# An mLSTM cell and a SwiGLU block on one core: scores and state products in one segment at a seam, and a mask by maximum

## The chip, the core and the metric

The kernel runs on one core of a Trainium2 chip. The core has a matrix engine (TensorE, PE in the profile; its weight loads are PEld), a vector engine (VectorE, DVE), an activation engine (ScalarE, ACT), a general engine (GpSimd, POOL) and a queue engine that issues DMAs (SyncE, SP). Each engine runs its own instructions in order, and semaphores order them between engines. The metric is the time of one execution in microseconds, as the median of several.

## The reference

An mLSTM cell runs over 768 time steps for 4 batches and 8 heads with 40 features a head, and its output is the input of a gated feed-forward block with 320 inputs and 1536 hidden units. Everything is in 32-bit floats, except the weights, which come as 64-bit floats.

```python
for t in range(S):                                   # cell
    m_new = maximum(f[t] + m, i[t])
    f_stab = exp(f[t] + m - m_new);  i_stab = exp(i[t] - m_new);  m = m_new
    C = f_stab * C + i_stab * outer(v[t], k[t])
    n = f_stab * n + i_stab * k[t]
    y[t] = sigmoid(o[t]) * (C @ q[t]) / max(|n . q[t]|, 1)
g = x @ w_gate                                       # block, x = y as (tokens, 320)
out = (g * sigmoid(g) * (x @ w_val)) @ w_out
```

## The kernel before

**The cell in stretches of 64 steps.** The recurrence is cut into sub-stretches of 64 steps. Inside one, the weight of key s for query t is a matrix: w = exp(g_s - M_t) for s up to t and 0 beyond, with g from the gates and M a running maximum. Then y is (scores * w) times v, plus the state from before, decayed. Two sub-stretches make a group of 128 steps, and there are six groups, each of 512 tokens (128 steps of 4 batches). For the cell of a group the kernel needs:
- the weights w: `weights_load` spreads M over w_sb by DMA (L476), `weights_sub` subtracts it from g on VectorE (L483), `weights_mask` writes -1e30 where s > t with an affine select on POOL (L488), and `weights_exp` takes the exponential on ScalarE (L492);
- `weigh_values` (L363, POOL): the values v times the last column of w, into vw_sb;
- kT and qT, keys and queries with features on partitions. For groups 2 on they are made from "squares": sixteen DMAs (`load_squares`, L336) bring k or q in squares of 32, and VectorE turns these in place (`turn_squares`, L342);
- `do_scores` (L352): 64 products of kT and qT; `do_weigh` (L359, VectorE) multiplies them by w;
- `do_add` (L378): 64 products of k_sb and vw_sb, what a sub-stretch adds to the state; `do_state` adds it (L394, VectorE), between decays of the state on POOL (L387, `do_decayed` for the first);
- `do_attend` (L401 and L406) and `do_gather` (L415 on): products with the state and with the values, summed and divided; `do_divide` and `send_squares` bring the result as squares to x_sq, where `turn_inputs` makes xT, the block's input.

**The block in two phases for each group.** From group 1 on, `gated` makes the hidden units in six chunks k of two blocks of 128. A seven-product scheme replaces eight block products, so there are sums of weights (`weight_sums`, made once, in group 1) and sums of inputs (`input_sums`, kept in q_sb). A chunk has products into a PSUM tile gv_x, then some into gv_y, then the rest into gv_x; `second(k - 1)` finishes the chunk before. `project_seven` then makes the outputs with seven products in steps 0 to 7. Group 0 goes another way: `hidden` for twelve blocks, and `project_all` with a list of things to do after each (`after`).

**The order is written out by hand.** While the block of group g runs, the cell of group n = g + 1 is computed and group f = g + 2 is loaded. The dictionary `at` says what is issued after which part of a chunk: "a" follows the first part of gv_x, "b" stands before gv_y, "c" behind gv_y, "d" at the chunk's end. So on TensorE `do_add` stands behind chunk 0 and `do_scores` behind chunk 1. `between(g)` does the same for the steps of `project_seven`. Each engine's queue follows this order.

**PSUM in four pairs.** From group 1 on, PSUM is four pairs of banks, handed out in turn: `take` takes the next free pair, and a pair goes back to the end of the list where the code says that its reader has been issued. gv_x and gv_y take one pair each, scores two, state products two. A product into a pair waits until the readers of its last use are through.

**Memory used twice.** x_sq holds the squares of the inputs, and its first part, under the name k_sq, the squares of k. POOL clears it once (`memset` in group 1). In group 0 the squares of k go to a tile of their own, "raw" (`early_squares`).

Of the kernel before, what the change touches and what calls it, by code (L numbers as in the profile page):

```python
# [9 lines left out]
F32 = mybir.dt.float32  # L10
# [3 lines left out]
AF = mybir.ActivationFunctionType  # L14
ALU = mybir.AluOpType
# [4 lines left out]
SUB = 64  # L20
NEG = -1e30
# [3 lines left out]
def kernel(  # L25
# [18 lines left out]
    nc = tc.nc  # L44
# [13 lines left out]
    UH = BH // 2  # L58
# [6 lines left out]
    const = ctx.enter_context(tc.tile_pool(name="const", bufs=1))  # L65
# [31 lines left out]
    def half(i):  # L97
        return slice(i * SUB, (i + 1) * SUB)
# [5 lines left out]
    def heads(P):  # L104
        return slice(P * UH, (P + 1) * UH)

    k_sb = const.tile([128, BH, DP], F32)
# [3 lines left out]
    w_sb = const.tile([128, BH, SUB], F32)  # L111
    vw_sb = const.tile([128, BH, D1], F32)
    kT = const.tile([128, PP, L], F32)
    qT = const.tile([128, PP, L], F32)
# [6 lines left out]
    g_T = const.tile([128, NG, BH], F32)  # L121
    e_T = const.tile([128, NG, BH], F32)
    dec = const.tile([128, NS - 2, PP], F32)
    tmp = const.tile([128, 3 * TW], F32)
    sw0 = const.tile([128, 3, 2, 128], F32)
    ident = early.tile([128, 128], F32)
    f0 = early.tile([128, L], F32)
    i0 = early.tile([128, L], F32)
# [215 lines left out]
    q_sq = q_sb.rearrange("p (a x) d -> p a (x d)", x=2).rearrange("p a (t d) -> p a t d", d=SQ)  # L344
# [3 lines left out]
    def scores(P):  # L348
        sp = [x.rearrange("p (a t) -> p a t", t=SUB) for x in duo("sp")]
        for a in range(UA):  # L350
            for two, i in QUAD:
                nc.tensor.matmul(sp[two][half(i), a, :], lhsT=kT[feats(two), P * UA + a, half(i)],  # L352
                                 rhs=qT[feats(two), P * UA + a, half(i)], start=True, stop=True)
        return sp

    def weigh(P, sp):
        w2 = w_sb[:, heads(P)].rearrange("p (a two) t -> p two a t", two=2)
        for two in range(2):
            nc.vector.tensor_tensor(w2[:, two], sp[two], w2[:, two], op=ALU.mult)  # L359
        give("sp", P)  # L360
# [11 lines left out]
    def add(n, P):  # L372
        ps = smalls("add")
        rows, w = (half, DP) if n == 1 else (feats, D)
        for a in range(UA):
            for i, two in QUAD:
                h = P * UH + 2 * a + two
                nc.tensor.matmul(ps[i][rows(two), a, :], lhsT=k_sb[half(i), h, 0:w], rhs=vw_sb[half(i), h, :],  # L378
                                 start=True, stop=True)
        return ps  # L380
# [104 lines left out]
    def weights_mask(P):  # L485
        for i in range(2):
            w = w_sb[half(i), heads(P)]
            nc.gpsimd.affine_select(w, w, compare_op=ALU.is_ge, fill=NEG, base=0, pattern=[[0, UH], [1, SUB]],  # L488
                                    channel_multiplier=-1)

    def weights_exp(P):
        nc.scalar.activation(w_sb[:, heads(P)], w_sb[:, heads(P)], AF.Exp)  # L492
# [13 lines left out]
    A, V, G = nc.scalar, nc.vector, nc.gpsimd  # L506
# [383 lines left out]
    def do_scores():  # L890
        for P in range(2):
            live["sp", P] = scores(P)

    def do_weigh(P):
        weigh(P, live.pop(("sp", P)))

    def do_add(n):
        for P in range(2):
            live["add", P] = add(n, P)
# [29 lines left out]
    def load_all(dst, a, n):  # L929
        for P in range(2):  # L930
            load(dst, a, n, P)

    run = lambda f, *a, **b: (lambda: f(*a, **b))
# [9 lines left out]
        1: [run(piece_load, 6), run(late_decay)],  # L943
        2: [run(nc.scalar.activation, step1, step1, AF.Exp), run(decay_rows), run(weights_load, 1), run(load_all, v_sb, v, 1)],
        3: [run(late_turns)],
        4: [run(decay)],
        5: [run(turn, 0, (A, A), (A, V))],
        6: [run(turn, 1, (A, A), (A, V)), run(piece_load, 7)],
        7: [run(weights_sub, 1, 0), run(weights_mask, 0), run(weights_sub, 1, 1), run(weights_mask, 1), run(nc.gpsimd.memset, q_sb, 0.0)],
        8: [run(weights_exp, 0), run(weights_exp, 1), run(weigh_values, G, 0), run(weigh_values, G, 1),  # L950
            run(piece_load, 8)],
# [11 lines left out]
    def early_squares(part):  # L963
# [10 lines left out]
        2: [run(do_divide, 1, 0), run(convert, 15)],  # L974
        3: [run(do_divide, 1, 1), run(load_all, o_sb, o_gate, 2), run(early_squares, 0), run(turn_squares, q_sq, qT)],
        4: [run(convert, 16), run(seam, 1, 0, (A, V, A, V))],
        5: [run(weights_sub, 2, 0), run(weights_mask, 0), run(seam, 1, 1, (A, V, A, V)), run(convert, 17)],
        6: [run(input_sums, V), run(load_all, k_sb, k, 2)],
        7: [run(weights_sub, 2, 1), run(weights_mask, 1), run(sig, 0), run(sig, 1)],
        8: [run(weights_exp, 0), run(weights_exp, 1), run(weigh_values, G, 0), run(weigh_values, G, 1)],  # L980
        10: [run(weight_sums, 0, V)],
        11: [run(early_squares, 1)],
    }
    project_all(0, after)
    early_scope.close()
# [6 lines left out]
    x_sq = late.tile([128, B * NKC, L // SQ, SQ], F32, name="x_sq")  # L992
    k_sq = x_sq.rearrange("p w t d -> p (w t d)")[:, 0:PP * L].rearrange("p (a t d) -> p a t d", a=PP, d=SQ)
# [4 lines left out]
    def loads_behind(f):  # L998
        return [run(load_all, v_sb, v, f), run(weights_load, f)]

    def between(g):
        n, f = g + 1, g + 2
        at = {i: [] for i in range(8)}
        if f < NG:
            at[0] += [run(load_squares, q_sq, q, f)]
        if n < NG:
            at[0] += [run(turn_inputs, n, u) for u in range(B)]
            at[1] += [run(double_inputs, n, u) for u in range(2)]
        if f < NG:
            at[1] += [run(load_squares, k_sq, k, f), run(load_all, k_sb, k, f)]  # L1010
            at[2] += [run(weights_sub, f, 0), run(weights_mask, 0), run(weights_sub, f, 1), run(weights_mask, 1)]
            if g == 1:
                at[1] = [run(out_weights, V, 2)] + at[1]
            at[4] += [run(weights_exp, 0), run(weights_exp, 1), run(sig, 0), run(sig, 1),
                      run(weigh_values, G, 0), run(weigh_values, G, 1), run(turn_squares, q_sq, qT)]
        if n < NG:
            at[4] += [run(input_sums, V)]
        if f < NG:
            at[7] += [run(turn_squares, k_sq, kT)]
        return at  # L1020

    for g in range(1, NG):
        n, f = g + 1, g + 2
        at = {}
        if n < NG:
            at["c", 0] = [run(do_decayed, 2 * n)]
            at["d", 0] = [run(do_add, n), run(do_state, 2 * n)]
            at["d", 1] = [run(do_scores), run(do_weigh, 0), run(do_weigh, 1)]
            at["d", 2] = [run(do_attend, n, 0), run(do_gather, n, 0)]
            at["c", 3] = [run(do_divide, n, 0), run(send_squares, 0)]  # L1030
            at["d", 3] = [run(do_attend, n, 1), run(do_gather, n, 1)]
            at["c", 4] = [run(do_divide, n, 1), run(send_squares, 1)]
        if f < NG:
            at["d", 3] += loads_behind(f)
            at["c", 4] += [run(load_all, o_sb, o_gate, f)]
        if g == 1:
            at["c", 2] = [run(nc.gpsimd.memset, x_sq, 0.0)]
            at["b", 4] = [run(out_weights, V, 0)]
            at["d", 4] = [run(out_weights, V, 3)]
            at["c", 5] = [run(out_weights, V, 1)]  # L1040
            for j in range(1, KH):
                at["a", j - 1] = at.get(("a", j - 1), []) + [run(weight_sums, j, G if j in (3, 4) else V)]
        gated(g, at)
        project_seven(g, between(g))
# [30 lines left out]
```

## Time and profile before

| what | us |
|---|---|
| median of 3 runs (515.2 to 516.48) | 515.66 |
| the profiled execution | 516.62 |
| its span, first to last instruction | 514.8 |
| granted TensorE clock | 0.998 |
| end of group 0's output products, start of group 1's gate products | 126.17 |
| group 1, from there to group 2's gate products | 79.94 |
| groups 2, 3 and 4, each | 78.4 |
| busy: PE, DVE, POOL, ACT | 506.3, 345.3, 279.2, 179.7 |

The page gives the busy time of each engine, the share of the chain of work that ended last, and groups of like instructions with their mean duration. A timeline row has the start, the time from the first to the last of a run of like instructions, the engine, the line, the operation, the tiles (out<-in), the shape and the number; what stands in brackets is idle time before it and what ended it. A TensorE row's length includes the last product's way through the array, so lengths of TensorE's segments are read here from start to start.

### The profile page before, as it was taken

The page shows a single profiled execution, that of the slowest core. Times are in us where ns is not written, and L with a number is a line of the kernel's source. Part 1 is how long each engine was busy: PE and PEld are TensorE (multiplying, and loading weights), DVE is VectorE, ACT ScalarE, POOL GpSimd, SP SyncE. Part 2 cuts the span into 40 slices and gives each one's busy share as a digit, 9 for nine tenths or more (in the row PEclk, how much of TensorE's full clock was granted, in tenths as well). Part 3 has the DMA queues.
Part 4 walks back from the last instruction along what each step waited for, and adds up shares of the span by engine and source line. Part 5 has one row for each costly group of instructions (what it writes and reads, how often), then busy time and mean ns, then how long its engine had stood idle before and what let it go on. Part 6 is the DMA issues. An engine that isn't in the chain of part 4 may idle for free.

```text
span 514.8 us, 14725 instructions
## 1 busy us (share of the span) xinstructions
PE 506.3 (98%) x6309; PEld 430.3 (84%) x6309; DVE 345.3 (67%) x547; ACT 179.7 (35%) x269; POOL 279.2 (54%) x283
## 2 busy tenths in 40 slices
PE   8999999999999999999999999999999999999997
PEld 4964445667888889898899898999898899988896
DVE  5779666899858879857669656659666754233421
ACT  3377555434222244322335322345231330123210
POOL 1303327566399789457657457657347750166710
PEclk9999999999999999999999999999999999999999
DMA  9999999698100866700886600896700210100001
GB/s 126 176 241 221 171 215 216 148 180 94 52 3 12 153 101 76 105 3 6 132 127 76 107 3 3 122 138 77 108 4 1 34 21 20 33 1 1 0 14 39
DMA packets 205497, 43.28 MB, mean 84 GB/s; under 512 B 193432, under 2 KB 200600, under 8 KB 205432
## 3 DMA queue, kind: packets, MB, share of 16 engines
q1 hardware_dynamic: 203444, 39.49, 47.7%
q10 hardware_dynamic: 1988, 2.85, 2.4%
q8 instruction: 50, 0.82, 0.7%
q14 instruction: 15, 0.12, 0.1%
HBM read 35.68 MB, written 4.01 MB: 77 GB/s over the span
## 4 chain that ended last, share of the span: by engine, by line
PE 77%; DVE 11%; POOL 4%; issue 3%; DMA 2%; ACT 2%; SPq 1%; DVEq 0%; ACTq 0%; POOLq 0%
PE gv_x L831 23%; PE o_ps L754 20%; PE gv_y L831 18%; PE gv_ps L683 5%; DMA w_sb<-M_dram 2%; PE inter L401 2%; PE intra L406 2%; PE sp L352 2%; PE first_y L562 1%; POOL w_sb L488 1%; PE burn L501 1%; DVE vw_sb L419 1%; POOL tmp L872 1%; PE tp_kq L541 1%; PE sp L551 1%
## 5 line engine op out<-in xcount | busy, mean ns | idle before, releaser
L831 PE MATMUL gv_x<-xT,wgv_sb 64*128 64x256 f32 x720 | 93.7, 382 | 0.7 <-ACT tmp L881 0.4
L831 PEld LDWEIGHTS gv_x<-xT,wgv_sb 64*128 64x128 f32 x720 | 69.0, 187 | 9.0 <-issue 1.1
L754 PE MATMUL o_ps<-wo_sb,h_sb 128*128 128x160 f32 x480 | 67.4, 300 | 0.0
L754 PEld LDWEIGHTS o_ps<-wo_sb,h_sb 128*128 128x128 f32 x480 | 65.6, 190 | 1.7 <-issue 1.7
L683 PE MATMUL gv_ps<-xT,wgv_sb 64*128 64x512 f32 x240 | 53.5, 595 | 0.3 <-DVE wgv_sb L228 0.3
L488 POOL TENSOR_SCALAR_AFFINE_SELECT w_sb<-w_sb 64x1024 f32<-64x1024 f32 x20 | 31.1, 1555 | 25.3 <-DVE w_sb L483 16.8
L683 PEld LDWEIGHTS gv_ps<-xT,wgv_sb 64*128 64x128 f32 x240 | 23.5, 187 | 25.0 <-issue 23.5
L831 PE MATMUL gv_y<-q_sb,wgv_sb 64*128 64x256 f32 x360 | 44.1, 377 | 0.3 <-DVE x_sb L871 0.3
L831 PE MATMUL gv_y<-xT,wgv_sb 64*128 64x256 f32 x360 | 44.0, 376 | 0.0
L879 ACT ACTIVATE h_sb<-gv_x 128x256 f32<-128x256 f32 x30 | 11.5, 384 | 86.3 <-PE gv_x L831 86.2
L831 PEld LDWEIGHTS gv_y<-q_sb,wgv_sb 64*128 64x128 f32 x360 | 35.3, 187 | 4.2 <-DVE x_sb L871 0.7
L831 PEld LDWEIGHTS gv_y<-xT,wgv_sb 64*128 64x128 f32 x360 | 35.5, 187 | 3.4
L754 PE MATMUL o_ps<-wT,S 128*128 128x160 f32 x240 | 33.5, 300 | 0.1
L754 PEld LDWEIGHTS o_ps<-wT,S 128*128 128x128 f32 x240 | 32.8, 190 | 0.4 <-DVE tmp L768 0.4
L871 DVE TENSOR_TENSOR tmp<-tmp,gv_y 128x1024 f32<-128x1024 f32 x15 | 18.3, 1220 | 20.2 <-PE gv_y L831 18.3
L872 POOL TENSOR_TENSOR tmp<-tmp 128x512 f32<-128x512 f32 x15 | 20.0, 1335 | 21.1 <-DVE tmp L871 21.1
L831 PE MATMUL gv_x<-q_sb,sw 64*128 64x256 f32 x240 | 31.0, 376 | 0.0
L852 POOL TENSOR_TENSOR h_sb<-tmp 128x512 f32<-128x512 f32 x13 | 16.7, 1287 | 25.5 <-ACT tmp L851 25.5
L871 DVE TENSOR_TENSOR x_sb<-x_sb,gv_y 128x1024 f32<-128x1024 f32 x15 | 18.3, 1218 | 17.0 <-PE gv_y L831 16.1
L861 ACT COPY tmp<-gv_x 128x1024 f32<-128x1024 f32 x15 | 15.2, 1012 | 40.5 <-PE gv_x L831 40.5
L721 POOL TENSOR_TENSOR S<-h_sb 128x256 f32<-128x256 f32 x30 | 22.8, 759 | 9.2 <-DVE h_sb L852 7.3
L723 POOL TENSOR_TENSOR S<-S,h_sb 128x256 f32<-128x256 f32 x30 | 27.3, 911 | 0.0
(216 smaller groups left out, 1004.2 us busy)
## 6 DMA issues: line engine op xcount, KB each, us to landing
w_sb<-M_dram SPq DMA_DIRECT2D x10, 512.0 KB, 7.3
k_sb<-in_k_dram SPq DMA_DIRECT2D x12, 320.0 KB, 6.5
v_sb<-in_v_dram SPq DMA_DIRECT2D x12, 320.0 KB, 5.8
o_sb<-in_o_gate_dram SPq DMA_DIRECT2D x12, 320.0 KB, 6.3
raw<-in_moe_w_out_dram SPq DMA_DIRECT2D x3, 1280.0 KB, 7.6
x_sq<-k_sb SPq DMA_DIRECT2D x64, 40.0 KB, 2.0
q_sb<-in_q_dram SPq DMA_DIRECT2D x32, 64.0 KB, 2.5
out_dram<-tmp SPq DMA_DIRECT2D x24, 80.0 KB, 2.8
```

Source lines behind the costliest of these rows:

```text
L352: nc.tensor.matmul(sp[two][half(i), a, :], lhsT=kT[feats(two), P * UA + a, half(i)], rhs=qT[feats(two), P * UA + a, half(i)], start=True, ...
L488: nc.gpsimd.affine_select(w, w, compare_op=ALU.is_ge, fill=NEG, base=0, pattern=[[0, UH], [1, SUB]], channel_multiplier=-1)
L683: nc.tensor.matmul(ps[i], lhsT=wgv_sb[half(i), m, kc, :], rhs=x[half(i), kc, :], start=(kc == 0), stop=(kc == NKC - 1))
L721: eng.tensor_tensor(S1[:, k], lo[:, second_half], hi[:, second_half], op=ALU.add)
L723: eng.tensor_tensor(S2[:, k], S1[:, k], lo[:, first_half], op=ALU.subtract)
L754: nc.tensor.matmul(node[x][:, i], lhsT=lhs(k)[:, ts(i, L)], rhs=rhs(k), start=start and k == 0 and i == 0, stop=stop and k == KH - 1, skip ...
L831: nc.tensor.matmul(ps[:, i, cols], lhsT=lhs(c)[half(i)], rhs=rhs(c)[half(i)], start=start and c == 0, stop=stop and c == n - 1, skip_group ...
L852: (nc.vector if k == KH - 1 else nc.gpsimd).tensor_tensor(h_sb[:, 2 * k + 1], uw[:, 0], uw[:, 1], op=ALU.mult)
L861: nc.scalar.copy(uw, x)
L871: nc.vector.tensor_tensor(uw, uw, y, op=ALU.add)
L872: nc.gpsimd.tensor_tensor(uw[:, :, second_half], uw[:, :, second_half], uw[:, :, first_half], op=ALU.add)
L879: nc.scalar.activation(h[:, first_half], x[:, 0, first_half], AF.Silu)
```

## The change

Four things are changed together.
- Scores and state products of the next group are issued at the seam, ahead of chunk 0 of `gated`, as one segment; the weighing follows at once, and `do_state` stands behind the first part of gv_x in chunk 0 ("a", 0). The decay before it moves to step 6 of `project_seven` ahead (for group 1: behind block 10 of `project_all`).
- The squares of k for group f are loaded at ("a", 0) and turned at the end of chunk 1 ("d", 1), no more in steps 1 and 7 of `project_seven`. The memset of x_sq stands ahead of group 1's first chunk. In `project_all` the turn of k moves from behind block 11 to block 9, and `weight_sums(0)` from 10 to 11.
- From group 2 on, the mask is a maximum on VectorE: w_sb, which holds M, is raised to +1e30 where s > t with a table `cap` made once on POOL. `weights_sub` and `weights_mask` go.
- The subtraction of M from g is done in the activation: exp(-w + g), with g as the bias, which is one value for each partition and head, so there are 32 activations of 128x64 in the place of two of 128x1024. They stand at step 3 of `project_seven`, `weigh_values` with them.

```diff
+    cap = const.tile([128, SUB], F32)
...
+    def cap_table():
+        nc.gpsimd.memset(cap, -3e38)
+        for i in range(2):
+            c = cap[half(i)]
+            nc.gpsimd.affine_select(c, c, compare_op=ALU.is_ge, fill=-NEG, base=0, pattern=[[1, SUB]],
+                                    channel_multiplier=-1)
+
+    def weights_cap(P):
+        w = w_sb[:, heads(P)]
+        nc.vector.tensor_tensor(w, w, cap.unsqueeze(1).to_broadcast([128, UH, SUB]), op=ALU.max)
+
+    def weights_bias(n, P):
+        for h in range(P * UH, (P + 1) * UH):
+            nc.scalar.activation(w_sb[:, h], w_sb[:, h], AF.Exp, bias=g_T[:, n, h:h + 1], scale=-1.0)
...
-        4: [run(decay)],
+        4: [run(decay), run(cap_table)],
...
-        5: [run(weights_sub, 2, 0), run(weights_mask, 0), run(seam, 1, 1, (A, V, A, V)), run(convert, 17)],
+        5: [run(weights_cap, 0), run(seam, 1, 1, (A, V, A, V)), run(convert, 17)],
         6: [run(input_sums, V), run(load_all, k_sb, k, 2)],
-        7: [run(weights_sub, 2, 1), run(weights_mask, 1), run(sig, 0), run(sig, 1)],
-        8: [run(weights_exp, 0), run(weights_exp, 1), run(weigh_values, G, 0), run(weigh_values, G, 1)],
-        10: [run(weight_sums, 0, V)],
-        11: [run(early_squares, 1)],
+        7: [run(weights_cap, 1), run(sig, 0), run(sig, 1)],
+        8: [run(weights_bias, 2, 0), run(weigh_values, G, 0), run(weights_bias, 2, 1), run(weigh_values, G, 1)],
+        9: [run(early_squares, 1)],
+        10: [run(do_decayed, 4)],
+        11: [run(weight_sums, 0, V)],
...
-            at[1] += [run(load_squares, k_sq, k, f), run(load_all, k_sb, k, f)]
-            at[2] += [run(weights_sub, f, 0), run(weights_mask, 0), run(weights_sub, f, 1), run(weights_mask, 1)]
+            at[1] += [run(load_all, k_sb, k, f)]
+            at[2] += [run(weights_cap, 0), run(weights_cap, 1)]
...
-            at[4] += [run(weights_exp, 0), run(weights_exp, 1), run(sig, 0), run(sig, 1),
-                      run(weigh_values, G, 0), run(weigh_values, G, 1), run(turn_squares, q_sq, qT)]
+            at[3] += [run(weights_bias, f, 0), run(weigh_values, G, 0), run(weights_bias, f, 1), run(weigh_values, G, 1)]
+            at[4] += [run(sig, 0), run(sig, 1), run(turn_squares, q_sq, qT)]
...
-            at[7] += [run(turn_squares, k_sq, kT)]
+            at[6] += [run(do_decayed, 2 * f)]
...
+        if g == 1:
+            nc.gpsimd.memset(x_sq, 0.0)
         if n < NG:
-            at["c", 0] = [run(do_decayed, 2 * n)]
-            at["d", 0] = [run(do_add, n), run(do_state, 2 * n)]
-            at["d", 1] = [run(do_scores), run(do_weigh, 0), run(do_weigh, 1)]
+            do_scores()
+            do_add(n)
+            do_weigh(0)
+            do_weigh(1)
+            at["a", 0] = [run(do_state, 2 * n)]
...
         if f < NG:
+            at["a", 0] += [run(load_squares, k_sq, k, f)]
+            at["d", 1] = [run(turn_squares, k_sq, kT)]
...
         if g == 1:
-            at["c", 2] = [run(nc.gpsimd.memset, x_sq, 0.0)]
```

## The prediction

> **What bounds the kernel now.** I read the page first, then the order of work on TensorE, then every engine at the first place that the change touches.
>
> ```profile
> PE 506.3 (98%) x6309; PEld 430.3 (84%) x6309; DVE 345.3 (67%) x547; ACT 179.7 (35%) x269; POOL 279.2 (54%) x283
> PE 77%; DVE 11%; POOL 4%; issue 3%; DMA 2%; ACT 2%; SPq 1%; DVEq 0%; ACTq 0%; POOLq 0%
> ```
>
> TensorE is busy for 98% of the span and holds 77% of the chain. What another engine saves counts only where TensorE waits for it; what shortens TensorE's own queue counts in full. So I looked at what the two segments that are moved cost there. This is TensorE's timeline in group 3:
>
> ```profile
> 290.63 0.60 PE L831 MATMUL gv_x<-xT,wgv_sb 64*128 64x256 f32 x4
> 291.16 1.48 PE L378 MATMUL add<-vw_sb,k_sb 64*40 64x41 f32 x128
> 292.86 1.14 PE L831 MATMUL gv_x<-xT,wgv_sb 64*128 64x256 f32 x8 [0.22 <-ACT tmp L881]
> ...
> 300.83 2.10 PE L352 MATMUL sp<-qT,kT 40*64 40x64 f32 x128
> ...
> 302.85 1.14 PE L831 MATMUL gv_x<-xT,wgv_sb 64*128 64x256 f32 x8
> ...
> 335.86 1.46 PE L831 MATMUL gv_x<-xT,wgv_sb 64*128 64x256 f32 x12
> ...
> 338.45 1.46 PE L831 MATMUL gv_y<-q_sb,wgv_sb 64*128 64x256 f32 x12
> ```
>
> The first number is the start. 24 gate products take 2.59 us where other gate products follow (335.86 to 338.45), and 2.69 where state products follow (288.47 to 291.16): entering 64-wide tiles costs 0.10. Leaving costs as much: 64 `inter` take 0.95 (310.82 to 311.78), the 64 `intra` behind them, with the return to gate products, 1.05. Besides, gv_x of chunk 1 stands idle for 0.22, since its PSUM pair comes back only after chunk 0's ScalarE and VectorE work.
>
> The other place is the first seam (end of group 0), on all engines:
>
> ```profile
> 123.28 1.85 SPq L137 DMA_DIRECT2D k_sb<-in_k_dram  x2
> 123.44 2.48 POOL L488 TENSOR_SCALAR_AFFINE_SELECT w_sb<-w_sb 64x1024 f32<-64x1024 f32 x2 [3.36 <-DVE w_sb L483]
> ...
> 125.95 1.06 ACT L492 ACTIVATE w_sb<-w_sb 128x1024 f32<-128x1024 f32 x1 [6.78 <-POOL w_sb L488]
> 126.00 2.80 POOL L363 TENSOR_TENSOR vw_sb<-v_sb,w_sb 128x656 f32<-128x656 f32 x2
> ...
> 126.17 1.13 PE L831 MATMUL gv_x<-xT,wgv_sb 64*128 64x256 f32 x8
> ...
> 127.56 2.36 DVE L342 STREAM_TRANSPOSE kT<-raw 128x1024 f32<-128x1024 f32 x2
> ```
>
> When the gate products start at 126.17, nothing that the moved segments read is there: no kT (turned at 127.56 to 129.92), no vw_sb (to 128.80), no k_sb (its two loads land 4.5 and 6.0 us after issue: 127.8 and 129.8). Today state products need them at 132.84, scores at 143.09. The change asks for them at 126.17.
>
> **The change part by part.**
>
> *One segment, groups 2 to 4.* From gv_x of chunk 0 to gv_x of chunk 2 group 3 takes 18.37 us (284.48 to 302.85). Gate products alone are 1.83 + 2.16 + 2.59 + 1.83 + 3.45 + 2.59 = 14.45, so the two excursions cost 3.92. In one segment: scores 2.02 less one exit 0.10, state products 1.70 less the idle 0.22, together 3.40, and about 0.05 for the entry from the output products (8 of group 0's, 0.275 each, take 2.35 before `inter`: 0.15; the entry to gate products, paid today, is 0.09: the last 12 before 284.48, 0.136 each, take 1.72). 3.45 against 3.92: 0.47 a group, three groups **-1.4 us**.
>
> What could stall there, with group 3's times: scores and state products take all four PSUM pairs, so gv_x waits for `weigh(0)`. Its scores are there at 285.7; VectorE's last output addition ends at 285.14; two of four multiplications (2.48) end at 287.0, and TensorE comes at 287.9: 0.9 to spare. gv_y waits for `weigh(1)` at 288.3 and is due at 289.8. `do_state` follows on VectorE (4.09, to 292.4): L871, ready at 292.1, is 0.3 late, and gv_x of chunk 1, which takes its pair, is due at 294.5. `do_decayed` (two of 0.735 on POOL) is done some 3 us before `do_state`. k_sb is issued at about 274.8 instead of 283.27, since 8.4 us of square loads leave the queue ahead of it; the output stores gain the same time. The squares, now behind the stores, start at about 287, take 8.4 and land 2.2 later, 297.6; their turn is due at about 302, with 2.37 in the place of the weighing's 2.48.
>
> *Mask and subtraction.* The maximum costs what the subtraction did (L483, 1.30 each). POOL loses 6.6 us of masks a group; nothing on TensorE waits for them in groups 2 to 4. Two exponentials of 1.06 become 32 of 64 elements:
>
> ```profile
> L492 ACT ACTIVATE w_sb<-w_sb 128x1024 f32<-128x1024 f32 x10 | 10.6, 1058 | 21.5 <-POOL w_sb L488 21.5
> L881 ACT ACTIVATE tmp<-tmp 128x256 f32<-128x256 f32 x15 | 6.3, 417 | 13.6 <-DVE tmp L880 13.6
> ```
>
> A 128x1 activation (L246) takes 203 ns, so the line through 417 and 1058 gives 0.257 at 64. Two sigmoids in a row take 1.36 where one takes 0.737: the second starts 0.1 before the first ends, so 0.16 from start to start. Bounds 0.16 and 0.42 (256 elements); I take 0.16 to 0.26, 5 to 8 us of ScalarE. In group 3 they start at 273.3 and end by 281.6; sigmoids follow to 284.2, POOL's second `weigh_values` ends by 283.0, needed at 287.1: 4 us to spare. The cap table (three POOL instructions at 53 us, a sixteenth of L488's size two of them) lies in an idle 2.6 us.
>
> *The first seam.* Without masks VectorE comes to `weights_cap(1)` 1.36 earlier (L220 and L221 at 115.42 took 0.99 and 1.63 beside a mask, 0.44 and 0.82 elsewhere) and ends it at 121.9; 16 activations to 124.6, `weigh_values` 126.0, `do_decayed` 127.5, then the 2.23 memset of x_sq (to 129.7, ahead of the decay that `do_state` asks of POOL at about 132). The last square lands at 124.9; kT is turned by 127.3; `weight_sums(0)`, behind it, 1.7 to 129.2; `weigh(0)` to 130.45. TensorE: scores 126.3 to 128.5, with a wait for kT's second half; first state products; the second half waits for k_sb at 129.8 and leaves at 130.65. So gv_x starts at **130.65**. With 14.45 of gate products chunk 2 starts at 145.10; today it does at 145.12 (where 0.58 in gv_y at 136.34 is lost to the late `do_state`, gone too). **0.0 us**: the saving is eaten by waits. Bounds: 130.35 if k_sb came at once, 132.5 if the memset held up VectorE.
>
> ```profile
> 155.45 2.23 POOL L933 MEMSET x_sq<- 128x2560 f32 x1
> ...
> 167.00 1.27 POOL L872 TENSOR_TENSOR x_sb<-x_sb 128x512 f32<-128x512 f32 x1
> ```
>
> ```profile
> 157.41 0.19 DVE L422 SCALAR_TENSOR_TENSOR den<-vw_sb 128x16 f32<-128x16 f32 x1
> ...
> 167.39 0.93 DVE L422 SCALAR_TENSOR_TENSOR den<-vw_sb 128x16 f32<-128x16 f32 x1
> ```
>
> The same VectorE instruction takes 0.19 inside the memset (to 157.68) and 0.93 beside L872, so I let the memset hold up nothing. [...]
>
> *Late group 1.* TensorE loses 0.98 us there: 24 gv_x at 178.15 take 3.05 (2.59), 12 gv_y 1.50 (1.39), the output phase 23.41 (23.02), 0.03 in between. The chain back is POOL and VectorE from 167 on, with VectorE held by POOL (0.93 above). The memset in chunk 2 goes, so POOL runs 0.6 earlier (it caught up by 158.8). I take **-0.3**, between 0 and -0.98.
>
> Sum: -1.4 + 0.0 - 0.3 = **-1.7 us**. The profiled run took 516.62 (span 514.8, 1.8 around it), 0.96 above the median 515.66. 514.9 on its own scale, **514.0** against the median.
>
> **The rivals.**
> - *The short activations cost what 256 elements cost* (slower). At 0.40 the first seam's end at 130.9, `weigh_values` at 132.3, gv_x starts at 133.15: +2.5. In groups 2 to 4 they end at 286.05, `weigh_values` at 287.5 against 287.1: +1.2 in all. With the -1.4, **517.9**. It breaks even at about 0.37. For it: no activation between 1 and 256 elements is in the trace. Against: 203 at one element. [...]
> - *The first seam is later*, by the memset or by squares or k_sb landing up to 2 us later: 132.5 instead of 130.65 gives back 1.85: **515.8**. For it: VectorE (130.45) and k_sb (130.65) end within 0.2 us of each other, so either can decide.
> - *All of late group 1's stalls go*: -1.4 - 0.98: **513.3**. For it: 2.2 us less on POOL and 2.48 of weighing out of chunk 1. Against: POOL had caught up before, and the turn of k comes in.
>
> **How the numbers follow.** 0.3% is 1.55 us, about what a measurement of this kernel can tell from no change: faster is below 514.1, slower above 517.2. Forecast 0.55, spread over 513.2 to 514.9, 0.33 of it below 514.1; late stalls gone 0.17; later seam 0.13; short activations 0.15. Faster 0.50, same 0.22 + 0.13 = 0.35, slower 0.15. The range 512.7 to 516.9 leaves out most of the short activations and a tail below.
>
> **What would show it.** In the profile after: groups 2 to 4 with scores and state products side by side, about 3.45 us from the end of output products to gv_x, no idle before that gv_x, none before gv_x of chunk 1; group 3 some 0.5 shorter than 78.4. At the first seam gv_x at 130.65 instead of 126.17, with waits for kT and k_sb. The 64-element activations between 0.16 and 0.26. Wrong would be: an idle gv_x behind `weigh(0)` in groups 2 to 4, a stall on the late turn of the squares, or a first seam past 132.

## The result, and the profile after

The changed kernel takes **522.33 us** (median of five runs, 521.73 to 524.0) against 516.48 for the kernel before on the same chip. The ratio is 1.0124, with a 95% interval of 1.0101 to 1.0148. The change is slower by some 6 us; the forecast was 514.0, which was -1.7 against the median before (515.66) that it started from.

| us | before | after |
| --- | --- | --- |
| profiled execution, its span | 516.62, 514.8 | 521.73, 519.9 |
| start to the end of group 0's output products | 126.23 | 128.41 |
| group 1, to the end of its output products | 79.94 | 79.78 |
| group 2 | 78.38 | 80.22 |
| group 3 | 78.38 | 78.91 |
| group 4 | 78.38 | 79.11 |
| group 5 and the end | 73.5 | 73.5 |

The page of the kernel after, busy time and the shares of the chain:

```profile
PE 506.0 (97%) x6307; PEld 433.9 (83%) x6309; DVE 335.4 (65%) x547; ACT 202.3 (39%) x389; POOL 256.0 (49%) x270
PE 89%; issue 3%; DVE 2%; DMA 2%; POOL 1%; ACT 1%; SPq 0%; DVEq 0%; ACTq 0%; POOLq 0%
```

VectorE's share of the chain fell from 11% to 2% and GpSimd lost 23 us, as the change meant. TensorE has as much work as before (506.0 against 506.3) in a span that is 5.1 longer. So the loss is idle time of TensorE, and the waits of TensorE name it (us in total, times, longest):

```profile
PE add L379 <- issue: 6.2, 4, 2.4
PE intra L407 <- issue: 1.7, 1, 1.7
```

"issue" means that TensorE waited for nothing that the profile shows: no semaphore, no other engine. The four times are the four merged segments. This is group 3's, on TensorE's timeline (start, length, rows):

```profile
284.97 3.42 PE L770 MATMUL o_ps<-wo_sb,h_sb 128*128 128x160 f32 x24
288.33 2.10 PE L353 MATMUL sp<-qT,kT 40*64 40x64 f32 x128
290.24 0.47 PE L379 MATMUL add<-vw_sb,k_sb 64*40 64x41 f32 x29
291.67 1.19 PE L379 MATMUL add<-vw_sb,k_sb 64*40 64x41 f32 x99 [0.96 <-issue]
292.79 1.14 PE L847 MATMUL gv_x<-xT,wgv_sb 64*128 64x256 f32 x8
293.76 1.03 PE L847 MATMUL gv_x<-q_sb,sw 64*128 64x256 f32 x8
```

Scores and state products stand side by side, gv_x follows without idle, but the state products stop for 0.96 us after 29 of their 128 rows. Nothing starts there: row 30 reads the same tiles as row 29. (The 64 products of each kind stand in the trace as 128 rows, two for each f32 product, and so do their weight loads.)

| segment of group | from scores to gv_x | idle marked issue, before row | without it |
| --- | --- | --- | --- |
| 1 | 128.34 to 133.34: 5.00 | 1.48, row 99 of 128 | 3.52 |
| 2 | 208.11 to 214.07: 5.96 | 2.44, row 128 | 3.52 |
| 3 | 288.33 to 292.79: 4.46 | 0.96, row 30 | 3.50 |
| 4 | 367.24 to 372.10: 4.86 | 1.29, row 59 | 3.57 |

Counted in rounds of 128 rows, the idle's place moves on by 29 or 30 rows from group to group: 99, 128, then 30 and 59 of the next round. A wait for data would not count rows. The first seam on all engines, as it came out:

```profile
119.88 7.75 ACT L505 ACTIVATE w_sb<-w_sb,g_T 128x64 f32<-128x64 f32 x32
...
125.45 2.37 DVE L343 STREAM_TRANSPOSE kT<-raw 128x1024 f32<-128x1024 f32 x2 [2.20 <-POOL vw_sb L364]
127.53 1.37 ACT L709 COPY x_sb<-o_ps 128x320 f32<-128x320 f32 x4
127.75 0.38 DVE L822 TENSOR_TENSOR sw<-wgv_sb 128x256 f32<-128x256 f32 x1
127.76 1.54 POOL L364 TENSOR_TENSOR vw_sb<-v_sb,w_sb 128x656 f32<-128x656 f32 x1 [2.52 <-ACT w_sb L505]
...
128.34 2.09 PE L353 MATMUL sp<-qT,kT 40*64 40x64 f32 x128
...
130.25 1.17 PE L379 MATMUL add<-vw_sb,k_sb 64*40 64x41 f32 x98
...
132.90 0.51 PE L379 MATMUL add<-vw_sb,k_sb 64*40 64x41 f32 x30 [1.48 <-issue]
```

kT was turned by 127.82 and the weighted values were there at 129.3, both before TensorE asked; the idle of 1.48 comes in the middle of the state products here too.

What I took to stop TensorE without a semaphore is the supply of its own program. The page has a queue for instructions, the same in both kernels:

```profile
q8 instruction: 50, 0.82, 0.7%
```

It fetches 50 packets of 16 KB. TensorE has 6307 product rows and 6309 weight loads in the trace, 12,616 in all: 252 for each packet. One packet is thus a page of about 256 instructions, or 128 product rows with their weight loads, and the idle in the segments is 128 rows apart, with the groups' other rows counted in. In group 2 the trace has the fetch from 210.81 to 212.34, and the idle ends at 213.92; in group 1 from 130.57 to 131.72 and 132.90. In all four segments the idle ends 1.2 to 1.6 us after such a fetch does; what fills that time the trace does not show. The state products use up 128 rows in 1.6 us, the scores in 2.0.

**Theory**: the merged segment of 256 short rows outruns the fetch of TensorE's program. **Rivals**: the mask part (32 short activations, a busier ScalarE) costs the time; a wait for data (k, weighted values, a PSUM pair) that the profile does not show as such.

### The profile page after: what moved, and what is told of

It is laid out like the page before. It is cut to its first block, busy times and chain, and to the rows that moved or that the text cites. A ratio compares the mean times of both kernels' runs of the same rounds, so it can differ in the third digit from the quotient of the medians.

```text
span 519.9 us, 14804 instructions
## 1 busy us (share of the span) xinstructions
PE 506.0 (97%) x6307; PEld 433.9 (83%) x6309; DVE 335.4 (65%) x547; ACT 202.3 (39%) x389; POOL 256.0 (49%) x270
## 4 chain that ended last, share of the span: by engine, by line
PE 89%; issue 3%; DVE 2%; DMA 2%; POOL 1%; ACT 1%; SPq 0%; DVEq 0%; ACTq 0%; POOLq 0%
PE gv_x L847 25%; PE o_ps L770 22%; PE gv_y L847 20%; PE o_ps L716 5%; PE gv_ps L699 5%; DMA w_sb<-M_dram 2%; PE inter L402 2%; PE intra L407 2%; PE sp L353 2%; PE add L379 1%; PE first_y L578 1%; POOL w_sb L489 1%; PE burn L517 1%; PE tp_kq L557 1%; PE sp L567 1%
## 5 line engine op out<-in xcount | busy, mean ns | idle before, releaser
L847 PE MATMUL gv_x<-xT,wgv_sb 64*128 64x256 f32 x720 | 92.0, 380 | 0.2 <-ACT x_sb L897 0.2
L847 PEld LDWEIGHTS gv_x<-xT,wgv_sb 64*128 64x128 f32 x720 | 70.4, 187 | 7.2 <-ACT x_sb L897 0.3
L699 PE MATMUL gv_ps<-xT,wgv_sb 64*128 64x512 f32 x240 | 53.5, 595 | 0.3 <-DVE wgv_sb L229 0.3
L699 PEld LDWEIGHTS gv_ps<-xT,wgv_sb 64*128 64x128 f32 x240 | 24.5, 187 | 24.1 <-issue 22.8
L364 POOL TENSOR_TENSOR vw_sb<-v_sb,w_sb 128x656 f32<-128x656 f32 x10 | 14.0, 1401 | 39.0 <-ACT w_sb L505 38.9
L505 ACT ACTIVATE w_sb<-w_sb,g_T 128x64 f32<-128x64 f32 x128 | 31.0, 333 | 0.0
L716 PE MATMUL o_ps<-wo_sb,h_sb 128*128 128x320 f32 x96 | 28.1, 451 | 0.0
```

Source lines behind the costliest of these rows:

```text
L364: eng.tensor_tensor(vw_sb[:, heads(P)], v_sb[:, heads(P)], w_sb[:, heads(P), last].to_broadcast([128, UH, D1]), op=ALU.mult)
L505: nc.scalar.activation(w_sb[:, h], w_sb[:, h], AF.Exp, bias=g_T[:, n, h:h + 1], scale=-1.0)
L699: nc.tensor.matmul(ps[i], lhsT=wgv_sb[half(i), m, kc, :], rhs=x[half(i), kc, :], start=(kc == 0), stop=(kc == NKC - 1))
L716: nc.tensor.matmul(ps[u], lhsT=hid(g, m)[:, ts(u, L)], rhs=wo_sb[:, m, :], start=(m == 0), stop=(m == NFC - 1))
L847: nc.tensor.matmul(ps[:, i, cols], lhsT=lhs(c)[half(i)], rhs=rhs(c)[half(i)], start=start and c == 0, stop=stop and c == n - 1, skip_group ...
```

## The experiments

**One part at a time.** e1_split takes the merge apart and keeps everything else:

```
             do_scores()
-            do_add(n)
             do_weigh(0)
             do_weigh(1)
-            at["a", 0] = [run(do_state, 2 * n)]
+            at["a", 0] = []
+            at["d", 0] = [run(do_add, n), run(do_state, 2 * n)]
```

> The changed kernel with the state products (and the state update behind them) back behind chunk 0 of the gate products; scores and weighing stay at the seam, the cap, the bias activations, the earlier turn of squares and all loads stay as in the change. Theory (TensorE's own program, fetched in pages of 256 instructions, does not keep up with 256 short products = 512 to 1024 instructions in one go): with 128 short products in a row no idle marked issue of over 0.5 us is left in scores or state products, groups 2 to 4 take about 78.3 us each (79 to 80.2 in the change), 515.5 us in all, or 517.7 if the 2.2 us that the change lost before the first seam belong to it. Rival (the mask and the short activations, or the moved queue work, cost the time): 520 to 522, nearly as the change.

Measured: 516.07 us against 516.31 for before, ratio 0.9994 (0.9974 to 1.0015). Groups 2 to 4 take 78.18 us each, and no idle is left in scores or state products:

```profile
283.76 2.10 PE L353 MATMUL sp<-qT,kT 40*64 40x64 f32 x128
285.78 1.13 PE L847 MATMUL gv_x<-xT,wgv_sb 64*128 64x256 f32 x8
...
292.46 1.59 PE L379 MATMUL add<-vw_sb,k_sb 64*40 64x41 f32 x128
294.15 1.13 PE L847 MATMUL gv_x<-xT,wgv_sb 64*128 64x256 f32 x8
```

The whole loss is in the merge. Group 0's output products end at 126.48 here, at 126.94 and 124.57 in the two runs below whose TensorE program is the same up to there, and at 128.41 in the change: the 2.2 us that the change lost ahead of the first seam are not a cost that its program always has: the end varies from execution to execution.

e2_mask does the opposite: the kernel before with the mask part alone.

```
-            at[2] += [run(weights_sub, f, 0), run(weights_mask, 0), run(weights_sub, f, 1), run(weights_mask, 1)]
+            at[2] += [run(weights_cap, 0), run(weights_cap, 1)]
...
-            at[4] += [run(weights_exp, 0), run(weights_exp, 1), run(sig, 0), run(sig, 1), ...
+            at[4] += [run(weights_bias, f, 0), run(weights_bias, f, 1), run(sig, 0), run(sig, 1), ...
```

> The kernel before with only the mask part of the change: table of caps, a maximum on VectorE in the place of subtraction and mask, 32 activations with bias in the place of two exponentials, at the places where those were; no segment moved. Theory (program supply in the merged segment): no difference, 516.5 give or take 0.8, the same idle in TensorE's timeline as before. Rival (the mask part costs the time): 519 to 522. If the 2.2 us lost before the first seam come from the table or the activations: 518.7.

Measured: 515.76, ratio 0.9989 (0.9966 to 1.0012). The mask part is neither a loss nor a gain that can be measured. Its span in the profile is 512.1 against 514.8, and 2.1 of that difference are an earlier first seam (124.11), a little below the spread just told (124.57 to 128.41).

e3_oldmask is the change with the old subtraction, mask and exponential.

```
-            at[2] += [run(weights_cap, 0), run(weights_cap, 1)]
+            at[2] += [run(weights_sub, f, 0), run(weights_mask, 0), run(weights_sub, f, 1), run(weights_mask, 1)]
...
-            at[3] += [run(weights_bias, f, 0), run(weigh_values, G, 0), run(weights_bias, f, 1), run(weigh_values, G, 1)]
+            at[3] += [run(weights_exp, 0), run(weigh_values, G, 0), run(weights_exp, 1), run(weigh_values, G, 1)]
```

> The changed kernel with the old subtraction, mask and exponential in the place of cap, maximum and bias; the merged segment and all moves stay. Theory (program supply in the merged segment): idle marked issue of 1 to 2.5 us in the middle of the state products in all four segments, as in the change; the first seam some 2 us later as the masks delay the weighted values; 522 to 526 in all. Rival (the mask part costs the time): the idle goes and it comes back to 515 to 518.

Measured: 524.64, ratio 1.0149 (1.0106 to 1.0193). The idle stays, at the same rows 99, 128, 30 and 59 (1.28, 1.84, 1.49, 1.87 us). The mask part is excluded as the cause.

**A gap.** e4_gap puts gv_x of chunk 0 between the scores and the state products.

```
-            do_add(n)
...
-            at["a", 0] = [run(do_state, 2 * n)]
+            at["a", 0] = [run(do_add, n), run(do_state, 2 * n)]
```

> The changed kernel with the state products behind gv_x of chunk 0 (1.83 us of gate products stand between scores and state products), ahead of the state update; all else as in the change. Theory (program supply): the 1.83 us give the fetch time for most of a page, so the idle marked issue in the segment falls from 1.0 to 2.4 us to 0.5 or less each; groups 2 to 4 about 78.1 us; 515.3 to 517.5 in all. Rival (a data wait that the profile does not show, on the weighted values or k): the state products come 2 us later, so that would go too, and this run alone does not tell them apart; rival (mask part or queues): 520 to 522.

Measured: 517.07, ratio 1.0023 (1.0002 to 1.0045). The idle fell to 0.3 or less in three of four groups. In group 3 1.48 us stayed, behind the state products:

```profile
286.53 1.59 PE L379 MATMUL add<-vw_sb,k_sb 64*40 64x41 f32 x128
288.06 0.91 PE L847 MATMUL gv_y<-q_sb,sw 64*128 64x256 f32 x5
290.45 0.48 PE L847 MATMUL gv_y<-q_sb,sw 64*128 64x256 f32 x2 [1.48 <-issue]
```

So the idle is not tied to state products either: here it stops long gate products, whose operands are the same before and behind it. I had expected 0.5 at most; a gap of 1.83 us is too small where a boundary falls badly.

**The supply by itself.** e5_probe appends runs of score products of several lengths to the kernel before; all their inputs have long been there.

```
+        long(16)
+        for n in (64, 128, 192, 256, 1024):
+            short(n)
+            long(16)
```

> The kernel before with a probe appended after its last group (nothing is left out; the probe's products are not used): runs of score products (128, 256, 384, 512 and 2048 TensorE rows, each row a weight load and a product, so 256 instructions for 128 rows) with 16 large products of 128x512 between them. Theory (the program is supplied in pages of 256 instructions, about 3 us from one page boundary to the next page's start): the run of 128 rows goes through in about 2.0 us with at most 0.5 us of idle; 256 rows show one idle of 1 to 2.4 us, 384 and 512 rows one or two more; the run of 2048 rows takes about 3 us per 128 rows, some 48 us in all, with idle marked issue at every 128th row. Rival (no limit of supply; the idle in the segment was a wait for data): 2.0 us per 128 rows throughout, 32 us for 2048 rows, no idle, since the probe's inputs have long been there.

```profile
525.63 2.09 PE L1033 MATMUL short<-qT,kT 40*64 40x64 f32 x128
...
541.59 3.01 PE L1033 MATMUL short<-qT,kT 40*64 40x64 f32 x186
545.69 1.27 PE L1033 MATMUL short<-qT,kT 40*64 40x64 f32 x70 [1.09 <-issue]
...
560.82 2.54 PE L1033 MATMUL short<-qT,kT 40*64 40x64 f32 x154
564.48 2.09 PE L1033 MATMUL short<-qT,kT 40*64 40x64 f32 x128 [1.11 <-issue]
568.22 3.05 PE L1033 MATMUL short<-qT,kT 40*64 40x64 f32 x102 [1.65 <-issue]
...
628.14 25.34 PE L1033 MATMUL short<-qT,kT 40*64 40x64 f32 x896 [0.34 <-issue]
```

128 rows go through in 2.02 us (525.63 to 527.65) with no idle. 256 rows take 5.30 instead of 4.0, and the longer runs stop again and again, 128 rows apart: 564.48 to 568.22 is **3.74 us for a page**, of which the array works 2.1. In that page the fetch is in the trace from 565.63 to 566.76, so it takes 1.13 of the 3.74; what fills the rest stays open. It is not other traffic on the DMA engines: from 559.90 to 566.73 the DMA engines' share was 0.02. That is 29 ns a row, where scores take 16 and state products 12.5. The rival, 2.0 us per 128 rows throughout, is out. I had said 3 us a page and 48 us for 2048 rows; they took 57.4 (615.61 to 672.98), near the 59.8 that 16 pages of 3.74 give. From 621.34 on the granted clock was 0.5 and the rows themselves took 28.3 ns (896 in 25.34), 3.6 us for 128, so the array was about as slow as the supply there, and little idle is left to see.

e6_twice issues the scores of chunk 1 twice in the kernel before, far from any seam.

```
-            at["d", 1] = [run(do_scores), run(do_weigh, 0), run(do_weigh, 1)]
+            at["d", 1] = [run(do_scores), run(do_scores_again), run(do_weigh, 0), run(do_weigh, 1)]
```

> The kernel before with the scores of groups 2 to 5 computed twice in a row at their place in chunk 1 (same inputs, same PSUM tiles): a short segment of 256 rows where there were 128, away from the seam. Theory (program supply): idle marked issue of 0.7 to 2.4 us appears inside the scores of each of the four groups, where before has none; the time is 516.4 plus 4 x 2.02 of work plus 4 x 1 to 2 of idle: 528 to 533 us. Rival (the idle of the change comes from the seam or from the state products' inputs): no idle in the scores, 524 to 525 us.

Measured: 531.75 against 517.36. Each is a single execution. Idle marked issue appears in the second scores in the gate products of groups 1, 2 and 4 (1.21, 1.52, 1.09). Group 3 has none, which the expectation had not allowed for. Group 1, then group 3:

```profile
147.41 0.81 PE L899 MATMUL sp<-qT,kT 40*64 40x64 f32 x39 [1.21 <-issue]
...
308.29 0.63 PE L831 MATMUL gv_x<-xT,wgv_sb 64*128 64x256 f32 x4
308.84 2.10 PE L352 MATMUL sp<-qT,kT 40*64 40x64 f32 x128
310.76 2.24 PE L899 MATMUL sp<-qT,kT 40*64 40x64 f32 x128
```

There the boundaries fall some 18 rows into each of the two scores (28 rows on from row 118 of group 2, in rounds of 128), and the fetch started at 308.43, before the scores did. My reading is that TensorE's sequencer had crossed the boundary while long gate products were still queued ahead; no row of the trace shows the crossing itself.

**Moving the boundaries.** e7_shift changes nothing but the count of instructions ahead of everything.

```
     burn(7)
+    t = bank("shift")
+    for _ in range(64):
+        nc.tensor.matmul(t[:, 0:16], lhsT=junk[:, 0:128], rhs=junk[:, 0:16], start=True, stop=True)
```

> The changed kernel with 64 tiny unused products (128 instructions) at the start of TensorE's program, which shifts every boundary between pages of 256 instructions by half a page, 64 rows of the segment; nothing else changes. They take some 2 to 4 us at the start. Theory (pages): the idle in the segment stays between 0.9 and 2.5 us but moves to other rows: group 1 from row 99 of the 128 state products to row 35, group 2 from row 128 to row 64, group 3 from row 30 to row 94, group 4 from row 59 to row 123 (give or take 3). Rival (a wait for data: weighted values, k, a PSUM pair): the idle stays at the rows 99, 128, 30 and 59, or its place has nothing to do with the shift.

```profile
128.30 0.54 PE L379 MATMUL add<-vw_sb,k_sb 64*40 64x41 f32 x35
130.27 1.12 PE L379 MATMUL add<-vw_sb,k_sb 64*40 64x41 f32 x93 [1.42 <-issue]
...
208.11 0.81 PE L379 MATMUL add<-vw_sb,k_sb 64*40 64x41 f32 x64
210.78 0.82 PE L379 MATMUL add<-vw_sb,k_sb 64*40 64x41 f32 x64 [1.85 <-DVE w_sb L360]
...
287.70 1.13 PE L379 MATMUL add<-vw_sb,k_sb 64*40 64x41 f32 x93
290.19 0.57 PE L379 MATMUL add<-vw_sb,k_sb 64*40 64x41 f32 x35 [1.36 <-issue]
...
366.86 1.41 PE L379 MATMUL add<-vw_sb,k_sb 64*40 64x41 f32 x122
370.78 0.28 PE L379 MATMUL add<-vw_sb,k_sb 64*40 64x41 f32 x6 [2.51 <-issue]
```

The idle now stands before rows 36, 65, 94 and 123; 35, 64, 94 and 123 were expected. (Group 2's 1.85 carries the name of VectorE's weighing in the profile. But in the change the same row 65 passed at 210.66 without idle, while the weighing still ran to 211.89; so that is not what it waits for, and it moved with the others.) A count of instructions moved the idle by 63 or 64 rows in every group, so no wait for data is left as an explanation. The one execution took 520.62.

**Can the boundaries be put where they cost nothing?** e8_tiny and e9_sem put them at about row 20 of scores and state products in all four segments, by one-column products or by increments of an unused semaphore; e10_sem64 puts them at row 64 as a control.

In e8_tiny, ahead of the output products of group 0 and of groups 1 to 3:

```
+        tiny(40, ps[0], hid(g, 0)[:, 0:L], wo_sb[:, 0, 0:1])
...
+            tiny(15, node["a"][:, 0], a11(0)[:, 0:L], wo_sb[:, 0, 0:1])
```

> The changed kernel with unused one-column products that only shift the boundaries between pages of 256 instructions: 40 (160 instructions) ahead of group 0's output products, 15 (60 instructions) ahead of the output products of groups 1 to 3, so that in all four merged segments the boundaries fall at about row 20 of the scores and row 20 of the state products. Theory (a page that is crossed while long products are still queued is asked for early, and the page after it holds long products again): hardly any idle marked issue is left, at most 0.5 us a segment, against 0.96 to 2.44; the products themselves cost TensorE about 4 us (a product 0.05 to 0.06 us by the 0.026 that half as many instructions took), and the time is still 4 to 6 us under the change: 516 to 518. Rival (the loss is in the change's other moves, or every place of the boundaries costs the same): the idle stays at 1 to 2.4 us, and the time is the change's plus 4: 525 to 527.

Measured: 549.99, ratio 1.0648 (1.0592 to 1.0704). My price for the product was wrong: a one-column f32 row with 128x128 weights takes 0.112 us (33 from 94.62 on), not 0.026 to 0.03, and 0.215 (42 from 98.20 on) where the granted clock is 0.5, as it was for 13.7 us here. Its 170 rows of that kind (80 in group 0, 30 in each of groups 1 to 3) hide what the run was to show in the total. In the segments the idle stands at row 18 or 19 of the state products in two groups (1.43 and 0.50, none in the others), and 0.94 to 1.15 of new idle behind it in three, among gate products.

e9_sem strews the increments among the output products, 158 in group 0 and 59 in each of groups 1 to 3; e10_sem64 has 70 in the place of 158.

```
+            nc.tensor.sem_inc(fill_sem)
```

> As the run with one-column products, but the boundaries are shifted by instructions that give the array no work: increments of an unused semaphore on TensorE's queue, 158 strewn among group 0's output products and 59 among the output products of each of the groups 1 to 3 (0.27 us of product between one and the next). Theory: the same place of the boundaries, at most 0.5 us of idle a segment, and, if the increments go by while products are still queued, no cost: groups 2 to 4 at 77.8 to 78.2 us against 78.4 before, 514.0 to 516.0 in all, which would be the gain that was forecast for the change. Rival: the increments hold up TensorE's queue by 0.05 us each (335 of them, 17 us), or the idle stays: 521 or more.

> The same with 70 in the place of the 158 increments, so that the boundaries fall at about row 64 of the scores and of the state products in all four segments; the groups' 59 stay. A control of the place with the same means. Theory: idle marked issue of 1.3 to 1.9 us at about row 64 of the state products in each of the four segments, 5 to 7 us in all, and a time 4 to 7 us above the run with 158. Rival (the increments themselves, not the place, did it): no idle, and the same time as that run.

e9_sem: 522.41, ratio 1.0118 (1.0083 to 1.0154). In its group 3:

```profile
288.01 2.10 PE L353 MATMUL sp<-qT,kT 40*64 40x64 f32 x128
289.92 0.39 PE L379 MATMUL add<-vw_sb,k_sb 64*40 64x41 f32 x19
290.49 1.30 PE L379 MATMUL add<-vw_sb,k_sb 64*40 64x41 f32 x109 [0.18 <-issue]
291.73 1.14 PE L860 MATMUL gv_x<-xT,wgv_sb 64*128 64x256 f32 x8
292.69 1.02 PE L860 MATMUL gv_x<-q_sb,sw 64*128 64x256 f32 x7
294.44 0.48 PE L860 MATMUL gv_x<-q_sb,sw 64*128 64x256 f32 x1 [0.73 <-issue]
```

The idle at row 20 shrank to 0 to 0.45, as expected, but a second one of 0.45 to 0.73 stands at the next boundary, among gate products: the page between holds 109 short rows, and 290.49 to 294.44 is again 3.95 us. A segment pays 0.7 to 1.2 us where the merge saves 0.4. The increments of groups 1 to 3 were free (output products 23.28, 23.02, 23.02; before 23.41, 23.02, 23.02); the 158 of group 0, five in a row, cost 4.3 (the last stretch of output products 17.44 instead of 13.12). Without those it would be 518.1, worked out, not run. e10_sem64: 523.28, one execution, idle at row 64 in all four segments (2.12, 1.79, 0.90, 1.30), 6.1 us where e9 has 3.5. The place came out as expected, the expected 4 to 7 us between the two totals did not: e10 spares most of the 4.3 in group 0.

**A better kernel?** e11_spaced is e1_split with the second attend step of group 0 one step later.

```
-        0: [run(do_attend, 1, 1), run(convert, 14), ...
+        0: [run(convert, 14), ...
-        1: [run(do_gather, 1, 1), run(weights_load, 2), ...
+        1: [run(do_attend, 1, 1), run(do_gather, 1, 1), run(weights_load, 2), ...
```

> The split kernel (state products behind chunk 0, all else as in the change), and in group 0 the second attend step goes one step of four output products later, so that 2.2 us more of long products stand between the two short runs there, where idle marked issue of 0 to 1.7 us was seen. Theory (program supply): no idle marked issue over 0.3 us anywhere after 90 us; against before some 0.2 us less in each of groups 2 to 4, 0.8 in group 1, and on average about 0.6 in group 0: 514.3 us (513.5 to 515.5), a ratio of 0.996 to 0.999, at the edge of what the measurement tells. Rival (group 0 is held by other waits behind the later attend step, its division and the seam): 516 to 518.

Measured: 517.82 against 515.70, ratio 1.0037 (1.0016 to 1.0059). No idle marked issue over 0.3 us is left, and the rival came in: the division and the seam behind it are late, so TensorE stands idle until the inputs are turned.

```profile
111.22 0.71 PE L472 MATMUL tp_x<-ident,x_sb 64*128 64x64 f32 x16
113.78 0.44 PE L472 MATMUL tp_x<-ident,x_sb 64*128 64x64 f32 x4 [1.84 <-DVE xT L144]
```

No version here beats the kernel before by more than the measurement tells; e2_mask and e1_split equal it.

## Why the prediction was wrong

- **In one segment: 3.45 us against 3.92.** This step failed. The sizes were right: without idle the segment takes 3.50 to 3.57, so entry, exit and both sets of products were within 0.12, and the merge does spare about 0.4. What it left out is TensorE's program: 256 short rows want two pages in 3.5 us, and a page came every 3.7 to 4.0 (3.74 in e5_probe, 3.95 in e9_sem). Idle of 0.96 to 2.44 stands where -0.47 was forecast; groups 2 to 4 came out at +3.1 in all instead of -1.4.
- **The warning was in the trace of before.** Its waits had this line, which the prediction did not ask about:

```profile
PE intra L406 <- issue: 1.2, 1, 1.2
```

  Two attend steps of 128 short rows, 2.35 us of long products apart: two short pages in a row, the same pattern at the one place where before had it. In e5_probe one short page alone passed without idle (128 rows in 2.02 us) and two in succession did not (256 rows in 5.30); among the long products of e1_split the waits of PE have one idle marked issue in all (0.5, L699, in group 0).
- **The covers held.** No gv_x waits behind `weigh(0)`, gv_y does not wait for `weigh(1)`, the squares are turned in time at their new place, the memset holds up nothing that shows: the four weighings that VectorE starts beside it (131.25 in the change, the memset from 130.99 to 133.22) take 2.47, as they do without one (2.48 in group 3 before), so the 1.85 us priced for a memset that holds up VectorE did not show here. Of the three signs named as proving the prediction wrong, idle behind `weigh(0)` and a late turn did not come. The third did, a first seam past 132: gv_x starts at 133.34. But what it stood for, waits for data at the seam, did not hold it there; it was late by 2.2 us of group 0 and by 1.48 of idle marked issue.
- **The first seam, 0.0.** gv_x was forecast 4.48 us after the end of the output products, with waits for kT and k. It came 5.00 after the scores' start, without those waits and with 1.48 of idle marked issue. e1_split, with an earlier seam, has no wait for kT either: its scores start at 126.41, gv_x at 128.44 (k is needed later there). The waits were overestimated, and the program's supply took what they would have left. From the seam's start to chunk 2 it is 19.35 against 18.95 before: +0.4 where 0.0 was forecast, and -1.1 without the idle.
- **Late group 1, -0.3.** The right way, and within its bounds, but twice the size taken: from chunk 2 to the next seam it is 60.42 (147.69 to 208.11) against 60.98 (145.12 to 206.10), -0.56. So group 1 as a whole came out at -0.16, near the forecast -0.3, by two misses of opposite sign; that is luck.
- **The short activations, 0.16 to 0.26.** Right: 32 take 7.75, 0.24 from start to start. The rival of 0.40 is out, and with it the slower case that I had priced. The slower case that came was on no list of rivals.
- **The rest of the difference.** Profile against profile, the segments' groups give +2.9 and the stretch ahead of the first seam +2.2, which the profiles of three other kernels with the same TensorE program up to there do not have (e1, e3, e4). In the medians a clock effect (below) probably takes the place of the latter: the granted clock over a run was 0.993 to 0.997 in all five of the change, against 0.998 in before's profile. One window of 3.41 us at half the clock takes 0.003 off that mean, so by this estimate each run of the change had one or two. Where they fell is known for the profiled one alone, so this part of the 6 us is argued, not shown.

## What to carry to other kernels

Count instructions, not only time: in these runs 128 f32 product rows with their weight loads, about 256 TensorE instructions, are a page (the idle of e5_probe stands 128 rows apart), and a stretch that used up two pages in succession faster than 3.74 (e5_probe) to 3.95 us (e9_sem) each stopped, wherever its data were, but for group 3 of e6_twice, where the fetch started at 308.43 and the short rows at 308.84. Before short products from two places are brought together, look for idle marked issue in the middle of a group of equal products in the trace at hand, and see what stands next to it. Long products between short ones were not waste here: with 6.68 us of them between scores and state products (e1_split, 285.78 to 292.46) no idle was left in either, without them 0.96 to 2.44 us a segment. That the program comes in meanwhile is my reading of it.

## What the runs showed of the hardware

**Half a clock after a stall.** In the change the granted clock fell to 0.5 for 3.41 us right behind a stall of TensorE; e5_probe has stretches at 0.5 of 6.83, 10.24 and 54.62 us, two, three and sixteen times that. These are two windows in a row of the change, at group 0's attend step (columns: stretch, its length, busy time of each engine, granted clock, DMA):

```profile
96.97:100.38 3.41, 1.75 (x103) 1.60 (x103) 2.50 (x7) 2.04 (x3) 1.48 (x1) 1.00 0.76 114
100.38:103.79 3.41, 3.37 (x31) 2.49 (x31) 2.32 (x6) 0.00 (x0) 1.29 (x2) 0.50 0.46 72
```

TensorE was busy for 1.75 of 3.41 us, and in the next 3.41 us it ran at half its clock: the 32 output products there take 10.01 us instead of 8.81. A stall of 1.70 thus cost 2.9. In the other runs with single half-clock windows (e3, e6, e10, e11) each followed a window in which TensorE was busy for 0.38 to 0.68 of the time (in e3_oldmask for 1.84, 1.92 and 1.54 of 3.41 us). Busy shares of 0.47 to 0.58 also passed without one (e7, e3, and the change, with 1.86 of 3.41 us from 209.61 on and a clock of 1.00 behind it), so what decides stays open. e11's window followed a wait of 1.84 us for VectorE, so here it was not only stalls of the program's supply that it followed.

**Busy was not enough here.** In e8_tiny the 80 one-column products from 94.0 on kept TensorE occupied with 0.2 us of idle in all, and the granted clock still went to 0.5 from 98.30 to 111.95: a product took 0.112 us up to 98.20 and 0.215 behind it, and the eight output products from 107.29 to 111.83 took 4.54, where before has 2.35.
